# Order edges between VectorE and GpSimd, and ScalarE's copies in two halves, in an agent-attention and expert kernel

## The chip, the cores and the metric

The kernel runs on one core of a Trainium2 chip. The metric is device time in microseconds (us), the median of several executions. Five engines work side by side, each with its own instruction queue, which it works off in order: TensorE (PE in the profile), VectorE (DVE), ScalarE (ACT), GpSimd (POOL) and SyncE (SP, which issues most of the transfers). An instruction waits for others by semaphores, and what stands behind it on its engine waits with it.

## The reference

Agent attention over four batches of 10,048 tokens (128 channels, 49 agents), then one expert out of 16 for every token, which is picked in two steps (a group of four, then one of its four experts):

```python
a2k = softmax(scale * agents @ k^T)          # 4 x 49 x 10048
agent_v = a2k @ v                            # 4 x 49 x 128
x = softmax(scale * q @ agents^T) @ agent_v  # 4 x 10048 x 128
g = argmax(x @ w_group);  e = argmax(x @ w_expert[g])      # for each token
out = weight(g) * weight(e) * relu(x @ w1[g, e]) @ w2[g, e]   # 128 -> 1024 -> 128
```

The weights are the softmax values of the choices. q, k and agents are drawn eight times wider than v.

## The kernel before

Products run in f16 on TensorE, and precision is kept by splitting an f32 value into an upper f16 part and a lower one, the f16 of what the upper part leaves. For keys and queries (names `xf`, `xh`, `xl`) ScalarE copies the f32 chunk to `xh` and GpSimd takes `xl = xf - xh`, in pieces of 256 columns; a chunk has 10 tiles of 128 tokens, so 1,280 columns and five pieces. For values (`vf`, `vh`, `vl`) ScalarE writes `vh`, and **VectorE** takes `vl = 16 vf - vh` in two pieces of 640 columns; for the exponentials of the scores (`S`, `sh`, `sl`) GpSimd takes `sl = S - sh` in two pieces and adds `S` up in two more. For the exponentials of the queries (`ef`) GpSimd writes their lower part into `rows`. All of these read both operands from SBUF.

Batches come in the order 1, 2, 3, 0. The first 110 us or so do batch 1's attention. From then on to about 600 us TensorE works off *expert units*: for one of three batches at a time, and tiles of 512 tokens, eight units a tile. A unit is two products into PSUM (`ph`), an eviction by ScalarE (`hh`, relu) and by VectorE (`hl`, its lower part), and later three products `po`; up to eight units (`LAG`) lie between a unit's `ph` and its `po`. `ph` has three PSUM buffers, so TensorE waits when the evictions fall more than that behind. Between units `advance` puts steps of *lanes*, Python generators that do the attention of the following batches: `k1`, `k2`, `k3` (keys, then values), `q0` to `q3` (queries), `a0` to `a3` (weights, and in `pick` the choice of a batch's main expert), `p3` (scatter of rows). A lane that yields a number rests for so many units; how much of VectorE's and ScalarE's work goes between two units is held down by counts of it (`RATE`). The library's scheduler then orders each engine's queue by the data and order edges and a model of times of its own. So one more instruction, or one more yield, moves the order all over this stretch.

`pick` chooses a batch's main expert with a row of tiny VectorE instructions on 128 x 16 elements: `coe` is written, then multiplied in place by `cog` (both operands in SBUF), and so on to `cei`, the expert's number, by which SyncE loads its weights (`w1f`, `w2f`). This happens twice, for batches 2 and 3. From about 600 us the fourth batch, sorted by expert, is worked off.

`wide[0]` is True until the expert units begin. In the trace nearly all instructions of VectorE, ScalarE and TensorE carry line L140 (a helper that counts work), so they are told apart by the names of what they write and read.

Of the kernel before, what the change touches and what calls it, by code (L numbers as in the profile page):

```python
# [13 lines left out]
AF = mybir.ActivationFunctionType  # L14
ALU = mybir.AluOpType
# [5 lines left out]
P = 128  # L21
B = 4
N = 10048
C = 128
NA = 49
NG = 4
# [29 lines left out]
HT = CT // 2  # L56
VS = 16.0
# [21 lines left out]
HOP = 2  # L79
# [68 lines left out]
def build(ctx, tc, qT, kT, v, agT, wr, w1, w2, cpk, out, cols):  # L148
    nc = tc.nc
    pool, sync = nc.gpsimd, nc.sync  # L150
    work = np.zeros(3)
    pe = Counted(nc.tensor, work, 0, 4.0, 0.42)
    vec = Counted(nc.vector, work, 1, 65.0, 1.04)
    act = Counted(nc.scalar, work, 2, 190.0, 0.83)
# [19 lines left out]
    wide = [True]  # L174
# [101 lines left out]
    def split_load(kind, b, ci, early=None):  # L276
        t0, t1 = chunks[ci]
        n = (t1 - t0) * P if kind == "q" else min(N, t1 * P) - t0 * P
        if (kind, b, ci) in halves:
            lane("q0")["done"] += halves.pop("work") if "work" in halves else 0.0  # L280
            yield HOP
            return halves.pop((kind, b, ci))
        xf = loaded.pop((kind, b, ci), None) if early is None else first_loads[kind, ci]
        if early is not None and kind == "k" and ci < NB:
            xh = wbuf[ci].bitcast(F16)[:, 2 * CT * P:3 * CT * P]
            xl = early.tile([P, CT * P], F16, name="xs", bufs=4)
        elif early is not None and kind == "k" and ci > len(chunks) - 3:
            xh, xl = [early.tile([P, CT * P], F16, name="xs", bufs=4) for _ in range(2)]
        else:
            if xf is None:  # L290
                xf = load(kind, b, ci)
            xh = wk.tile([P, CT * P], F16, name="xh", tag="xh")
            xl = wk.tile([P, CT * P], F16, name="xl", tag="xl")
        act.activation(xh[:, 0:n], xf[:, 0:n], AF.Copy)
        if early is None:
            yield HOP
        a = 0
        if early is not None and kind == "k":
            a = min(n, SHARED)
            vec.tensor_sub(out=xl[:, 0:a], in0=xf[:, 0:a], in1=xh[:, 0:a])  # L300
        if a < n:
            for a in range(a, n, GP):
                z = min(n, a + GP)
                pool.tensor_sub(out=xl[:, a:z], in0=xf[:, a:z], in1=xh[:, a:z])  # L304
        return xh, xl

    chosen = []
# [9 lines left out]
    def paced(ins):  # L317

        tc.add_manual_dep(ins.ins, latest[0].ins.name, mybir.DependencyInfo(mybir.DependencyClass.Sync, mybir.DependencyReason.DATA),
                          reason="transfers are spread over the expert units")  # L320

    def skewed(n, *stages):

# [164 lines left out]
    def value_split(b, ci):  # L488

        st = state[b]  # L490
        vf = st.pop(("v", ci))
        sh, sl = [mo.tile([P, CT, NA], F16, name=name) for name in ("sh", "sl")]
        vh, vl = [wk.tile([P, CT * P], F16, name=name, tag="x" + name[1]).rearrange("p (t c) -> p t c", c=C) for name in ("vh", "vl")]
        parts = value_parts(b, ci)
        for x, y, m in parts:
            tc.keep_in_program_order(act.activation(vh[0:m, y], vf[0:m, y, 0:C], AF.Copy, scale=VS))
        yield 1
        for x, y, m in parts:
            act.activation(sh[0:m, y], x, AF.Copy)
        yield  # L500
        for x, y, m in parts:
            for a in range(0, x.shape[1], HT):
                z = slice(a, min(x.shape[1], a + HT))
                vec.scalar_tensor_tensor(out=vl[0:m, y][:, z], in0=vf[0:m, y, 0:C][:, z], scalar=VS, in1=vh[0:m, y][:, z], op0=ALU.mult, op1=ALU.subtract)
                yield
        yield 1
        for x, y, m in parts:
            for a in range(0, x.shape[1], HT):
                z = slice(a, min(x.shape[1], a + HT))
                pool.tensor_sub(out=sl[0:m, y][:, z], in0=x[:, z], in1=sh[0:m, y][:, z])  # L510
        for x, y, m in parts:
            for a in range(0, x.shape[1] if ci else 0, HT):
                z = slice(a, min(x.shape[1], a + HT))
                o = st["S"][0:m, y][:, z]
                pool.tensor_add(out=o, in0=o, in1=x[:, z])
        yield
        st["v", ci] = sh, sl, vh, vl

# [301 lines left out]
    def query_split(b, ci, x, early):  # L820
# [14 lines left out]
        x0 = st["rows", r][:, t0 - r * ST:t1 - r * ST]  # L835
        ef = x["ef"][:, 0:t1 - t0]
# [5 lines left out]
        if early:  # L842
            vec.tensor_sub(out=x0[:, :, NA:2 * NA], in0=ef, in1=x0[:, :, 0:NA])
        else:
            for a in range(0, t1 - t0, HT):
                z = min(t1 - t0, a + HT)
                pool.tensor_sub(out=x0[:, a:z, NA:2 * NA], in0=ef[:, a:z], in1=x0[:, a:z, 0:NA])  # L847
        st["split", ci] = True
        yield
        if b != SORTED and (t1 % ST == 0 or t1 == NT):  # L850
# [53 lines left out]
    def pick(b):  # L904
# [19 lines left out]
        og = sm.tile([P, NG], F32, name="cog")  # L924
# [3 lines left out]
        oe = sm.tile([P, NG, 4], F32, name="coe")  # L928
        vec.tensor_tensor(out=oe, in0=le, in1=em.unsqueeze(2).broadcast_to([P, NG, 4]), op=ALU.is_ge)
        yield  # L930
        vec.tensor_mul(out=oe, in0=oe, in1=og.unsqueeze(2).broadcast_to([P, NG, 4]))
        sc = sm.tile([P, NE], F32, name="csc")
        vec.tensor_sub(out=sc, in0=oe.rearrange("p g e -> p (g e)"), in1=eid)
        top = sm.tile([P, 1], F32, name="ctop")
# [917 lines left out]
```

## Time and profile before

| | |
|---|---|
| median of 3 runs | 914.24 us (911.54 to 914.42) |
| the profiled execution | 907.38 us, of which the profile's span is 905.1 us |
| TensorE busy, granted clock | 844.7 us (93%), 0.982 of full speed |
| VectorE, ScalarE, GpSimd busy | 710.8, 613.8 and 462.9 us (79%, 68%, 51%) |
| instructions | 22,546 |

Busy time is the union of an engine's instructions. An engine's idle time is put down to what ended it ("releaser"). TensorE's granted clock has two levels here, full speed (2.4 GHz, shown as 1.00) and half (1.2 GHz, 0.50); a stretch that has some of both shows a value between.

### The profile page before, as it was taken

The numbers are of one execution on the slowest core, as the hardware profiler recorded it, in microseconds if no ns is written. First come the engines' busy times: TensorE is split into PE (matmuls) and PEld (weight loads), VectorE is DVE, ScalarE is ACT, GpSimd is POOL, SyncE is SP. The second block draws the span as 40 slices with busy tenths as digits, with TensorE's granted clock in tenths as the row PEclk, the third lists the DMA queues.
The fourth block names the chain that finished last, engine by engine and source line by source line (L and its number), as shares of the span: only waits on it lengthen the run. The fifth ranks groups of instructions, "written<-read, shape, count | busy, mean of one in ns | idle before, by whom it ended". The sixth has DMA issues, their size and how long they took to land.

```text
span 905.1 us, 22546 instructions
## 1 busy us (share of the span) xinstructions
PE 844.7 (93%) x8668; PEld 502.2 (55%) x8669; DVE 710.8 (79%) x1442; ACT 613.8 (68%) x1078; POOL 462.9 (51%) x616
## 2 busy tenths in 40 slices
PE   4889999999797999898999999999999999999995
PEld 3745455555354555454455555554444477777775
DVE  7767898886799886688989689799977666766663
ACT  6568897867486777677678787766565555555552
POOL 4387495446426451838474343646555214444454
PEclk9989999999899999999999999999999999999998
DMA  9677436453554564434536222334756445555542
GB/s 360 245 244 272 139 108 225 157 163 128 173 170 130 169 196 147 156 115 152 169 112 242 83 75 104 112 102 151 230 176 212 138 140 165 174 190 187 176 141 98
DMA packets 58578, 149.95 MB, mean 166 GB/s; under 512 B 8702, under 2 KB 19830, under 8 KB 58460
## 3 DMA queue, kind: packets, MB, share of 16 engines
q1 hardware_dynamic: 53307, 138.11, 45.4%
q0 software_dynamic: 5152, 10.30, 3.2%
q8 instruction: 70, 1.15, 0.5%
q14 instruction: 49, 0.39, 0.1%
HBM read 108.33 MB, written 38.71 MB: 162 GB/s over the span
## 4 chain that ended last, share of the span: by engine, by line
PE 41%; DVE 8%; ACT 3%; DMA 2%; issue 2%; POOL 2%; POOLq 0%; ACTq 0%; DVEq 0%
PE po L140 24%; PE ph L140 12%; PE at L140 6%; DVE hl L140 3%; POOL xl L304 1%; ACT hh L140 1%; DMA out<-oo,er 1%; DVE vl L140 1%; DMA vf<-v 1%; DVE mq L140 1%; DVE ef L140 1%; ACT vh L140 1%; DVE oo L140 0%; POOL out L1485 0%; ACT es L140 0%
## 5 line engine op out<-in xcount | busy, mean ns | idle before, releaser
L140 DVE SCALAR_TENSOR_TENSOR hl<-ph,hh 128x512 f16<-128x512 f32 (+1 forms) x562 | 374.6, 677 | 125.7 <-ACT hh L140 122.0
L140 ACT ACTIVATE hh<-ph 128x512 f16<-128x512 f32 (+1 forms) x562 | 330.0, 594 | 188.2 <-PE ph L140 110.5
L140 PEld LDWEIGHTS <-wbuf 128*128 128x128 f16 (+2 forms) x2812 | 241.2, 97 | 282.6 <-issue 50.3
L140 PE MATMUL ph<-et,wbuf 98*128 98x512 f16 (+2 forms) x1048 | 317.4, 378 | 17.7 <-DVE hl L140 17.1
L140 PE MATMUL po<-hh,wbuf 128*128 128x512 f16 (+1 forms) x960 | 287.2, 379 | 0.0
L304 POOL TENSOR_TENSOR xl<-xf,xh 128x256 f16<-128x256 f32 x278 | 183.2, 696 | 137.1 <-ACT xh L140 124.4
L140 PE MATMUL po<-hl,wbuf 128*128 128x512 f16 (+1 forms) x480 | 181.3, 378 | 0.0
L1485 POOL DMA_INDIRECT out<-oo,er x82 | 80.7, 984 | 110.7 <-ACT hh L140 53.0
L140 PE MATMUL po<-wbuf,hh 128*128 128x128 f16 x1312 | 116.6, 219 | 0.0
L1199 POOL DMA_INDIRECT sorted_rows<-rows,slot x79 | 79.0, 1000 | 67.7 <-ACT hh L140 47.1
L140 PE MATMUL po<-wbuf,hl 128*128 128x128 f16 x656 | 112.9, 219 | 0.0
L140 PEld LDWEIGHTS <-hh 128*128 128x128 f16 x1312 | 99.2, 98 | 9.0 <-issue 9.0
L140 ACT ACTIVATE xh<-xf 128x1280 f16<-128x1280 f32 (+2 forms) x58 | 72.5, 1255 | 17.2 <-PE at L140 12.2
L510 POOL TENSOR_TENSOR sl<-S,sh 128x245 f16<-128x245 f32 (+2 forms) x51 | 37.8, 764 | 53.5 <-ACT sh L140 53.5
L140 PEld LDWEIGHTS <-hl 128*128 128x128 f16 x656 | 64.2, 98 | 0.0
L847 POOL TENSOR_TENSOR rows<-ef,rows 128x245 f16<-128x245 f32 (+1 forms) x62 | 39.9, 666 | 42.8 <-ACT rows L140 42.8
L140 PEld LDWEIGHTS <-xh 128*128 128x128 f16 x1166 | 46.3, 98 | 21.6 <-issue 2.2
L140 DVE SCALAR_TENSOR_TENSOR hl<-at,hh 128x512 f16<-128x512 f32 x82 | 55.8, 680 | 0.0
L140 DVE SCALAR_TENSOR_TENSOR vl<-vf,vh 128x640 f16<-128x640 f32 (+2 forms) x51 | 48.4, 956 | 7.2 <-ACT vh L140 7.2
L140 ACT ACTIVATE et<-at 98x512 f16<-98x512 f16 (+3 forms) x81 | 47.4, 596 | 8.8 <-PE at L140 8.7
L140 ACT ACTIVATE hh<-at 128x512 f16<-128x512 f32 x82 | 49.5, 604 | 0.0
L140 DVE TENSOR_TENSOR oo<-po,oo 128x512 f32<-128x512 f32 (+1 forms) x60 | 40.3, 672 | 9.6 <-PE po L140 6.2
(330 smaller groups left out, 1042.8 us busy)
## 6 DMA issues: line engine op xcount, KB each, us to landing
wbuf<-wdr SPq DMA_DIRECT2D x22, 832.0 KB
vf<-v SPq DMA_DIRECT2D x28, 645.0 KB
xf<-qT SPq DMA_DIRECT2D x27, 640.0 KB
xf<-kT SPq DMA_DIRECT2D x25, 640.0 KB
cols<-oo SPq DMA_DIRECT2D x60, 256.0 KB
oo<-cwt SPq DMA_DIRECT2D x57, 256.0 KB
erow<-rows SPq DMA_DIRECT2D x12, 490.0 KB
er<-sorted_rows SPq DMA_DIRECT2D x19, 256.0 KB
```

The source lines that it names most:

```text
L140: ins = f(*a, **k)
L304: pool.tensor_sub(out=xl[:, a:z], in0=xf[:, a:z], in1=xh[:, a:z])
L510: pool.tensor_sub(out=sl[0:m, y][:, z], in0=x[:, z], in1=sh[0:m, y][:, z])
L847: pool.tensor_sub(out=x0[:, a:z, NA:2 * NA], in0=ef[:, a:z], in1=x0[:, a:z, 0:NA])
L1199: ins = pool.indirect_dma_start(out=sorted_rows[:, :], out_offset=bass.IndirectOffsetOnAxis(ap=at, axis=0), in_=x, in_offset=None, bounds_ ...
L1485: ins = pool.indirect_dma_start(out=out, out_offset=bass.IndirectOffsetOnAxis(ap=to, axis=0), in_=y, in_offset=None, bounds_check=N - 1, o ...
```

## The change

`shared` marks GpSimd's pieces that read two operands from SBUF, and `by_itself` marks the `vl` pieces and the in-place product `coe` on VectorE. A `by_itself` instruction waits, by a semaphore edge, for the last `shared` piece that was issued before it in the program's order, unless another one has taken that edge; the next `shared` piece that is issued waits for the last `by_itself` instruction. Each mark is used up by its first taker. And after the opening, ScalarE's copy of a key or query chunk to `xh` is made in two halves of 640 columns, with a yield of one unit behind each, where one copy and a yield of two (`HOP`) stood.

```diff
-        act.activation(xh[:, 0:n], xf[:, 0:n], AF.Copy)
-        if early is None:
-            yield HOP
+        if early is None and not wide[0]:
+            for a in range(0, n, HT * P):
+                z = min(n, a + HT * P)
+                act.activation(xh[:, a:z], xf[:, a:z], AF.Copy)
+                yield 1
+            yield HOP - 1
+        else:
+            act.activation(xh[:, 0:n], xf[:, 0:n], AF.Copy)
+            if early is None:
+                yield HOP
...
-                pool.tensor_sub(out=xl[:, a:z], in0=xf[:, a:z], in1=xh[:, a:z])
+                shared(pool.tensor_sub(out=xl[:, a:z], in0=xf[:, a:z], in1=xh[:, a:z]))
...
+    lower, alone = [None], [None]
...
+    def follows(ins, other, reason):
+        tc.add_manual_dep(ins.ins, other.ins.name, mybir.DependencyInfo(mybir.DependencyClass.Sync, mybir.DependencyReason.DATA), reason=reason)
...
+    def shared(ins):
+
+        if alone[0]:
+            follows(ins, alone[0], "GpSimd pauses while VectorE reads both operands from SBUF")
+            alone[0] = None
+        if not wide[0]:
+            lower[0] = ins
+
+    def by_itself(ins):
+
+        if lower[0]:
+            follows(ins, lower[0], "VectorE reads both operands from SBUF when GpSimd pauses")
+            lower[0] = None
+        if not wide[0]:
+            alone[0] = ins
...
-                vec.scalar_tensor_tensor(out=vl[0:m, y][:, z], in0=vf[0:m, y, 0:C][:, z], scalar=VS, in1=vh[0:m, y][:, z], op0=ALU.mult, op1=ALU.subtract)
+                by_itself(vec.scalar_tensor_tensor(out=vl[0:m, y][:, z], in0=vf[0:m, y, 0:C][:, z], scalar=VS, in1=vh[0:m, y][:, z], op0=ALU.mult, op1=ALU.subtract))
...
-                pool.tensor_sub(out=sl[0:m, y][:, z], in0=x[:, z], in1=sh[0:m, y][:, z])
+                shared(pool.tensor_sub(out=sl[0:m, y][:, z], in0=x[:, z], in1=sh[0:m, y][:, z]))
...
-                pool.tensor_add(out=o, in0=o, in1=x[:, z])
+                shared(pool.tensor_add(out=o, in0=o, in1=x[:, z]))
...
-                pool.tensor_sub(out=x0[:, a:z, NA:2 * NA], in0=ef[:, a:z], in1=x0[:, a:z, 0:NA])
+                shared(pool.tensor_sub(out=x0[:, a:z, NA:2 * NA], in0=ef[:, a:z], in1=x0[:, a:z, 0:NA]))
...
-        vec.tensor_mul(out=oe, in0=oe, in1=og.unsqueeze(2).broadcast_to([P, NG, 4]))
+        by_itself(vec.tensor_mul(out=oe, in0=oe, in1=og.unsqueeze(2).broadcast_to([P, NG, 4])))
```

**The first choice of an expert.** GpSimd's queue before, where batch 2's `coe` is made on VectorE (numbers are buffers; "waits" names the engines and transfers whose semaphores an instruction waits for; x4 stands for four equal instructions):

```order
L847 TENSOR_TENSOR rows_3995<-ef_3824,rows_3995 128x5x49
L304 TENSOR_TENSOR xl_3795<-xf_3739,xh_3794 128x256 [waits DMAHW6_49,PE_49,Activation_49]
L304 TENSOR_TENSOR xl_3795<-xf_3739,xh_3794 128x256 x4
L304 TENSOR_TENSOR xl_3862<-xf_3807,xh_3861 128x256 [waits DMAHW6_49,PE_49,Activation_49]
L304 TENSOR_TENSOR xl_3862<-xf_3807,xh_3861 128x256 x4
L304 TENSOR_TENSOR xl_3957<-xf_3876,xh_3956 128x256 [waits DMAHW7_49,PE_49,Activation_49]
L304 TENSOR_TENSOR xl_3957<-xf_3876,xh_3956 128x256 x4
L304 TENSOR_TENSOR xl_4056<-xf_3977,xh_4055 128x256 [waits DMAHW0_49,PE_49,Activation_49]
L304 TENSOR_TENSOR xl_4056<-xf_3977,xh_4055 128x256 x4
```

And the same place of GpSimd's queue in the changed kernel:

```order
L311 TENSOR_TENSOR xl_3696<-xf_3597,xh_3695 128x256 x2
L875 TENSOR_TENSOR rows_4037<-ef_3851,rows_4037 128x5x49 [waits DMAHW3_49,Activation_49]
L875 TENSOR_TENSOR rows_4037<-ef_3851,rows_4037 128x5x49
L311 TENSOR_TENSOR xl_3776<-xf_3698,xh_3775 128x256 [waits DMAHW4_49,Activation_49]
L311 TENSOR_TENSOR xl_3776<-xf_3698,xh_3775 128x256 [waits Activation_49]
L311 TENSOR_TENSOR xl_3776<-xf_3698,xh_3775 128x256 x2
L311 TENSOR_TENSOR xl_3776<-xf_3698,xh_3775 128x256 [waits DVE_49]
L311 TENSOR_TENSOR xl_3566<-xf_3290,xh_3565 128x256 [waits DMAHW6_49,PE_49,Pool_49]
```

The first piece of the chunk `xl_3776` now stands behind the other four and waits for VectorE (for `coe`). VectorE's queue there, before and changed:

```order
L140 TENSOR_TENSOR oo_3591<-po_3593,oo_3591 128x512 [waits DMAHW7_49,DMAHW5_49,PE_49]
L140 TENSOR_REDUCE cem_3910<-at_3836 128x4
L140 TENSOR_TENSOR coe_3912<-at_3836,cem_3910 128x16 [waits DVE_49]
L140 TENSOR_TENSOR coe_3912<-coe_3912,cog_3908 128x16 [waits DVE_49]
L140 SCALAR_TENSOR_TENSOR hl_3897<-ph_3893,hh_3896 128x512 [waits Activation_49]
```

The same product in the changed kernel, which waits for GpSimd as well:

```order
L140 TENSOR_REDUCE cem_3823<-at_3752 128x4
L140 TENSOR_TENSOR coe_3825<-at_3752,cem_3823 128x16 [waits DVE_49]
L140 TENSOR_TENSOR coe_3825<-coe_3825,cog_3821 128x16 [waits DVE_49,Pool_49]
L140 TENSOR_TENSOR csc_3828<-coe_3825,cp_97 128x16 [waits DVE_49]
L140 TENSOR_REDUCE ctop_3830<-csc_3828 128x1 [waits DVE_49]
```

GpSimd's piece for which it waits is the last of `xl_3696`, two chunks ahead of it in program order.

**A value chunk's lower parts.** GpSimd's queue before at the first value chunks of batch 3; `sl` waits for ScalarE (`sh`) alone:

```order
L847 TENSOR_TENSOR rows_3995<-ef_4338,rows_3995 128x5x49
L510 TENSOR_TENSOR sl_4465<-S_3565,sh_4464 128x245 [waits Activation_49]
L510 TENSOR_TENSOR sl_4465<-S_3565,sh_4464 128x245
L515 TENSOR_TENSOR S_3565<-S_3565 128x245 [waits Pool_49] x2
L515 TENSOR_TENSOR S_3565<-S_3565 128x245 [waits Activation_49,Pool_49]
```

The same chunks of the changed kernel:

```order
L538 TENSOR_TENSOR sl_4793<-S_3592,sh_4792 128x245 [waits Activation_49]
L543 TENSOR_TENSOR S_3592<-S_3592 128x245 [waits Activation_49,Pool_49]
L543 TENSOR_TENSOR S_3592<-S_3592 128x245 [waits Pool_49]
...
L862 MEMSET rows_5878 128x98 [waits PE_49]
L875 TENSOR_TENSOR rows_4978<-ef_4874,rows_4978 128x5x49 [waits Activation_49]
L538 TENSOR_TENSOR sl_4793<-S_3592,sh_4792 128x245 [waits DVE_49]
L538 TENSOR_TENSOR sl_4906<-S_3592,sh_4905 128x245 [waits PE_49]
```

The first piece of `sl_4793` has moved behind the second, and waits for VectorE's `vl_4795`, the same chunk's.

**The load of batch 3's expert.** SyncE's queue before, and in the changed kernel:

```order
L1465 DMA oo_8119<-cwt1_141 128x512 [waits DMAHW7_49,DMAHW6_49,DMAHW1_49]
L1304 TENSOR_LOAD cei_7879 [waits DVE_49]
L1307 ISA
L1307 DMA w1f_8007<-w1 128x1024 [waits DMAHW0_49,Activation_49,Pool_49]
L1308 ISA
L1308 DMA w2f_8008<-w2 128x8x128 [waits DVE_49,Activation_49]
```

The changed kernel's, where the load takes the buffer that the chunk `xl_7406` gives back:

```order
L1493 DMA oo_8334<-cwt1_141 128x512 [waits DMAHW7_49,DMAHW0_49]
L1332 TENSOR_LOAD cei_7638 [waits DVE_49]
L1335 ISA
L1335 DMA w1f_7747<-w1 128x1024 [waits Pool_49]
L1336 ISA
L1336 DMA w2f_7748<-w2 128x8x128 [waits DMAHW3_49,DMAHW2_49,Activation_49]
```

And GpSimd's queue there in the changed kernel:

```order
L538 TENSOR_TENSOR sl_7863<-S_5984,sh_7862 128x147
L538 TENSOR_TENSOR sl_7863<-S_5984,sh_7862 64x49 [waits Activation_49]
L311 TENSOR_TENSOR xl_7406<-xf_7136,xh_7405 128x256 [waits DMAHW0_49,PE_49]
L311 TENSOR_TENSOR xl_7406<-xf_7136,xh_7405 128x256 x3
L311 TENSOR_TENSOR xl_7406<-xf_7136,xh_7405 128x256 [waits DVE_49]
```

The piece that gives the buffer free waits for VectorE's `vl_7865`; before, the load waited for pieces that stood far ahead of it.

## Rows read from the trace of the kernel before

**Rows 1.** Busy time by stage: us, each engine's busy us (instructions), clock, DMA.

```profile
110.00:600.00 490.00, 459.94 (x4541) 252.09 (x4541) 409.34 (x796) 368.49 (x641) 261.75 (x383) 0.98 0.44 147
600.00:880.00 280.00, 280.00 (x2820) 178.96 (x2819) 208.84 (x430) 162.48 (x303) 128.85 (x130) 1.00 0.51 170
```

**Rows 2.** TensorE's waits from 110 to 600 us: total us, times, longest.

```profile
PE ph L140 <- DVE hl L140: 16.7, 12, 5.6
PE at L140 <- POOL xl L304: 6.3, 7, 2.8
PE at L140 <- DVE vl L140: 1.5, 3, 0.6
```

**Rows 3.** TensorE's timeline: start, us, what; in brackets idle time before, releaser.

```profile
226.18 0.28 PE L140 MATMUL at<-agh,xl 128*128 128x49 f16 x5
232.03 1.01 PE L140 MATMUL ph<-et,wbuf 98*128 98x512 f16 x2 [5.56 <-DVE hl L140]
...
289.00 0.80 PE L140 MATMUL ph<-et,wbuf 98*128 98x384 f16 x2 [2.44 <-DVE hl L140]
...
383.97 0.30 PE L140 MATMUL at<-agh,xl 128*128 128x49 f16 x5 [2.81 <-POOL xl L304]
...
430.48 0.59 PE L140 MATMUL ph<-et,wbuf 98*128 98x512 f16 x2 [3.24 <-DVE hl L140]
```

**Rows 4.** VectorE's timeline at four places.

```profile
172.47 0.82 DVE L140 SCALAR_TENSOR_TENSOR vl<-vf,vh 128x640 f16<-128x640 f32 x1 [0.47 <-ACT vh L140]
...
224.15 7.22 DVE L140 TENSOR_TENSOR coe<-coe,cog 128x16 f32<-128x16 f32 x1
...
284.91 3.57 DVE L140 SCALAR_TENSOR_TENSOR vl<-vf,vh 128x640 f16<-128x640 f32 x1
...
447.86 2.46 DVE L140 SCALAR_TENSOR_TENSOR vl<-vf,vh 128x640 f16<-128x640 f32 x2
```

**Rows 5.** GpSimd's timeline around the same places, and at 375 us.

```profile
218.73 12.61 POOL L304 TENSOR_TENSOR xl<-xf,xh 128x256 f16<-128x256 f32 x20
...
283.47 3.18 POOL L304 TENSOR_TENSOR xl<-xf,xh 128x256 f16<-128x256 f32 x5
286.61 1.19 POOL L510 TENSOR_TENSOR sl<-S,sh 128x245 f16<-128x245 f32 x2
...
375.70 9.47 POOL L304 TENSOR_TENSOR xl<-xf,xh 128x256 f16<-128x256 f32 x15 [4.08 <-ACT xh L140]
...
447.80 1.84 POOL L510 TENSOR_TENSOR sl<-S,sh 128x245 f16<-128x245 f32 x2 [4.89 <-ACT sh L140]
```

**Rows 6.** Busy time behind the long waits, columns as in rows 1.

```profile
231.00:237.50 6.50, 5.47 (x27) 2.35 (x27) 6.21 (x22) 1.76 (x4) 0.34 (x1) 0.50 0.32 85
...
289.00:292.00 3.00, 3.00 (x25) 1.88 (x25) 3.00 (x6) 0.95 (x2) 0.00 (x0) 0.50 0.56 157
...
384.50:387.90 3.40, 3.40 (x23) 1.67 (x22) 2.02 (x4) 2.42 (x5) 3.40 (x7) 0.50 0.69 216
```

**Rows 7.** Groups by form from 110 to 600 us: busy us, mean ns, idle before.

```profile
L140 DVE SCALAR_TENSOR_TENSOR vl<-vf,vh 128x640 f16<-128x640 f32 x45 | 45.6, 1019 | 7.2 <-ACT vh L140 7.2
L140 DVE TENSOR_TENSOR coe<-coe,cog 128x16 f32<-128x16 f32 x2 | 7.5, 3775 | 0.1
...
L140 ACT ACTIVATE hh<-ph 128x512 f16<-128x512 f32 x316 | 186.3, 598 | 60.1 <-PE ph L140 57.5 <-DVE hl L140 0.9
L140 ACT ACTIVATE xh<-xf 128x1280 f16<-128x1280 f32 x36 | 45.7, 1272 | 15.5 <-PE at L140 11.1 <-POOL xl L304 2.4 <-DVE vl L140 1.0
...
L304 POOL TENSOR_TENSOR xl<-xf,xh 128x256 f16<-128x256 f32 x204 | 136.2, 704 | 120.5 <-ACT xh L140 108.2 <-PE at L140 9.8 <-DMA vf<-v 2.5
```

**Rows 8.** First load of an expert's weights, and TensorE's wait for it.

```profile
45.82 0.36 SPq L1307 DMA_DIRECT2D w1f<-w  x1
...
49.52 2.05 PE L140 MATMUL at<-w1f,at 128*128 128x512 f32 x2 [0.66 <-DMA w1f<-w]
```

**Rows 9.** `sl` over the whole span: duration ns min/median/max, first and last start.

```profile
L510 POOL TENSOR_TENSOR sl<-S,sh x51: 271/647/1286, 111.2 to 456.9; 128x245 f16<-128x245 f32 x45, 128x147 f16<-128x147 f32 x3, 64x49 f16<-64x49 f32 x3
```

## The prediction

> **What bounds the kernel now.** I read the busy time by stage first. From 600 to 880 us TensorE is busy all of the time, and from 110 to 600 us, where the change is at work, for 459.94 of 490 us [rows 1]: what can be won is the 30 us that TensorE idles there, and what half clock adds to them. VectorE is busy for 409 us of that stretch and ScalarE for 368, so neither is a bound over the whole, but each works its queue off in order, and one late instruction holds all that stand behind it. TensorE's own waits there come next: 16.7 us for `hl`, VectorE's eviction, in only twelve waits, and 6.3 us for GpSimd's `xl` [rows 2]. TensorE's timeline shows that four waits make up most of it, of 5.56, 2.44, 2.81 and 3.24 us [rows 3].
>
> I then looked at what VectorE did in the first two. From 224.15 us it spent 7.22 us on `coe`, a product of 16 columns whose other instance in the stretch took 0.3 us (two of mean 3,775 ns), and from 284.91 us 3.57 us on a `vl` piece that takes 0.82 where GpSimd is idle [rows 4, 7]. GpSimd was running pieces without a break: twenty `xl` from 218.73 to 231.34 us, and five `xl` and two `sl` from 283.47 to 287.80 [rows 5]. `coe` ended when the last of the twenty had ended, `vl` 0.68 us after the last `sl`. VectorE's instruction with two operands in SBUF was held for as long as GpSimd's back-to-back pieces lasted. In most other places it lost only the piece that was running: at 447.86 us two `vl` took 2.46 us where 1.64 are due, and GpSimd's two `sl` took 1.84 us in sum [rows 4, 5]. The third long wait is GpSimd's backlog itself, 15 pieces in a row from 375.70 us [rows 5], and the fourth I put down to neither part of the change.
>
> A long wait costs a second time. Behind the first, TensorE's granted clock was 0.50 for 6.5 us, behind the second for 3.0, behind the third for 3.4 [rows 6], and TensorE was busy there, so half of that is lost: 3.2, 1.5 and 1.7 us.
>
> **The change part by part.** The sum is made against the profiled execution's 907.4 us (span 905.1). The median of the runs is 914.24, 6.8 us above it, and I carry the difference over.
>
> *`coe` (gain).* Wait and clock are 5.56 + 3.2 = 8.8 us. In the changed queue `coe` waits for the last piece of a chunk that stands ahead of two `rows` pieces and four `xl` pieces, and the next piece after these waits for `coe`. So GpSimd can no longer run past it: at worst those six pieces lie in the way, at 12.61 / 20 = 0.63 us each, 3.8 us; at best nothing. The `ph` buffers cover a little over a unit, and most of the six are issued well ahead, so I take 1.3 us as left: -7.5. Bounds -8.8 and -4.
>
> *The long `vl` (gain).* 2.44 + 1.5 = 3.9 us. Only the first piece issued behind a `vl` is tied to it; the other four of an `xl` chunk are not, and in the changed queue they now stand ahead of the tied one. So a burst beside `vl` can come again, only shorter: -2.5, bounds -3.9 and 0.
>
> *The other `vl` (gain).* 45 pieces at 1,019 ns against 0.82 us are 9.0 us too much [rows 7, 4], of which the long one is 2.75. The other 6.2 us lie on VectorE and mostly under the three `ph` buffers; what reaches TensorE is near the 1.5 us that it waits for `vl` by name [rows 2]: -1.5, bounds 0 and -4.
>
> *Copies in halves.* A copy of 512 columns takes 598 ns and one of 1,280 takes 1,272 [rows 7], so 0.88 ns a column, and a half of 640 about 0.71 us by that line (an estimate). GpSimd may start 0.56 us sooner, and of TensorE's seven waits for `xl` I count four that begin with a fresh copy: 4 x 0.56, -2.0, bounds 0 and -6.3 - 1.7 = -8. ScalarE pays 2 x 0.71 - 1.27 = 0.15 us for each of 52 copies, 7.8 us. That lies in its idle quarter (368.49 of 490 us busy) and costs nothing as long as the halves go between evictions; without that cover it is up to +7.8. In the other direction, an eviction is held by a copy for 0.71 us at most where it was 1.27, which I put at nothing since no long wait of TensorE goes back to it.
>
> *GpSimd's `sl` behind `vl` (loss).* Before, `sl` ran beside `vl` and nobody waited for it: TensorE's waits for GpSimd name `xl` alone [rows 2]. Now the first piece of `sl` starts when the chunk's last `vl` has ended, and TensorE's first product with it reads just that piece. So `sl` comes up to 0.82 us later plus its own 0.65 [rows 4, 9]. There are 24 value chunks, and in the changed queue TensorE's first product with `sl` stands within a unit of the delayed piece in eight. I take 0.4 us each, +3; bounds 0 and 8 x 1.47 = 12. What is queued behind the piece on GpSimd, further `sl`, `S` sums and `xl`, is late by the same.
>
> *VectorE behind GpSimd (loss).* 12 of the `vl` and one `coe` wait for a piece of GpSimd's. Ten of the pieces are issued many units ahead; in two cases the piece stands directly ahead of the `vl`, behind a chunk of five pieces, 5 x 0.63 = 3.2 us. Behind the `vl` stand `hl` evictions, for which TensorE waits. +1.5, bounds 0 and 6.4.
>
> *The load of batch 3's expert (loss).* It now waits for the buffer of `xl_7406`, whose last piece waits for the last `vl` of batch 3. The first such load was issued at 45.82 us, and TensorE waited for it until 49.52, 3.7 us later [rows 8]. In the changed queue TensorE has other work between the issue and the product that needs the load, which I put at half of that: +2, bounds 0 and 3.7 + 1.7 for a half clock behind it = 5.4.
>
> *The new order elsewhere.* The extra instructions and yields move side work between units over the whole stretch, so waits such as those at 383.97 and 430.48 us [rows 3] may go or come again elsewhere. I take nothing for it, and up to 6 us either way in the range.
>
> The sum: -7.5 - 2.5 - 1.5 - 2.0 + 3 + 1.5 + 2 = -7.0 us. The profiled execution would come to about 900, the median to **907**.
>
> **A rule against a row.** At `coe` the row shows a wait through eleven or more pieces of GpSimd's [rows 4, 5]. The Trainium skill (SBUF — State Buffer, Who interferes with whom) says that a VectorE instruction with two SBUF inputs contends with a GpSimd instruction that reads SBUF, and that whichever comes second is blocked until the first has finished. That two such instructions exclude each other agrees with the rows; that the loser waits for one instruction does not: by that rule `coe` would have lost at most one piece, 0.66 us.
>
> **The rivals.**
> *GpSimd's pauses become the bound (slower).* The place is the value chunks: `sl` behind `vl`, and the `xl` of the other lane behind both, in a queue that had bursts of 9.47 and 12.61 us without a break [rows 5], in which every pause is handed on. If all 24 chunks lose the 0.65 us of a piece, that is 15.6 where I took 3, and the sum is +5.6; 920, and with one half clock more 921 to 922. It decides from about 0.42 us a chunk: 24 x 0.42 = 10 is what the gains of 13.5 leave after the other losses of 3.5. For it speaks that nothing on TensorE's side was moved back to make room; against it, that TensorE waited for `vl` only three times in 24 chunks [rows 2], so its products with values mostly come later than their operands.
> *The exclusion leaks (no change).* Four of five `xl` pieces stay untied. If `coe` and `vl` meet bursts as before, the gains of 11.5 us shrink to 4 or so, the copies' 2 and the losses of 6.5 stay, and it ends at 912 to 917. Against it: at `coe` the queue is fenced by a tied piece.
> *One piece only.* If VectorE loses but the piece that runs, then the 7 us of `coe` have a cause that the edges don't touch; the edges give 4.0 at most, and with the copies and the losses, -4.0 - 2.0 + 6.5, it ends near 915. The rows of GpSimd's burst, whose end is `coe`'s end within 0.03 us, speak against it. This is what the rule of the Trainium skill above would make of the change.
> *More is gained.* `xl` is late no more either, and the long waits at 383.97 and 430.48 us go too, the first with the half clock behind it [rows 6]: 2.8 + 1.7 + 3.2 = 7.7 us more, 894 to 902, or a little below.
>
> **How the numbers follow.** 907 has a chance of 0.46 with a range of its own of 902 to 911.5; more gained 0.18; the leak 0.14 and one piece only 0.04, both ending within 0.3% (911.5 to 917), which is about what a measurement of this kernel can tell from no change; GpSimd's pauses 0.18. So faster 0.64, same 0.18, slower 0.18. The range of 897 to 919 leaves out the better half of the fourth case and the worse half of the slower one.
>
> **What would show it.** Right: `coe` under 2 us in both places, no `vl` over 1.5 us, GpSimd's pieces beside them at 0.65 us and not 1.2, no half clock between 215 and 245 us, `xl` pieces starting within 0.75 us of their copy's start, and TensorE idle for 20 to 25 us from 110 to 600 us. Wrong: TensorE's waits name `sl`, or `w1f`'s load, for more than 6 us together; a `hl` that waits behind a `vl` which waits for GpSimd; or a new wait of over 2 us with half clock behind it at a place where before had none.

## The result and the profile after

The changed kernel took 918.8 us (median of 20 runs, 913.16 to 925.81), the kernel before, timed beside it, 912.97 us (20 runs, 908.84 to 915.33). The ratio is 1.0072 with a 95% interval of 1.0052 to 1.0091: slower by 0.7%, where I had forecast 0.8% faster. Its profiled execution has a span of 915.0 us against 905.1.

Busy time by stage, with the columns of [rows 1]:

```profile
110.00:600.00 490.00, 457.10 (x4466) 249.27 (x4464) 398.27 (x786) 367.19 (x675) 258.08 (x383) 0.98 0.45 145
600.00:880.00 280.00, 279.37 (x2796) 176.77 (x2794) 208.80 (x433) 162.48 (x303) 129.91 (x132) 1.00 0.51 170
215.00:245.00 30.00, 29.29 (x322) 16.06 (x320) 23.35 (x50) 23.73 (x45) 22.94 (x38) 1.00 0.65 208
281.60:285.00 3.40, 3.24 (x24) 1.92 (x25) 0.56 (x1) 2.14 (x3) 1.83 (x4) 0.50 0.62 195
428.40:435.10 6.70, 5.74 (x40) 2.82 (x40) 2.89 (x7) 1.26 (x3) 2.06 (x5) 0.50 0.59 222
476.20:479.50 3.30, 3.30 (x6) 1.20 (x6) 0.96 (x3) 1.59 (x3) 3.30 (x6) 0.50 0.73 234
```

TensorE idles 33 us from 110 to 600 us, where it idled 30. The place of the first choice, 215 to 245 us, now has under 1 us of idle time and no half clock. But half clock stands in the last three stretches, each behind one of the new waits below, and over the whole stretch the granted clock is 0.98 in both kernels: as much half clock came as went. TensorE's waits from 110 to 600 us say who is waited for:

```profile
PE ph L140 <- DVE hl L140: 6.3, 8, 2.2
PE at L140 <- POOL sl L538: 5.5, 5, 2.4
PE at L140 <- DVE ef L140: 4.3, 2, 2.6
PE at L140 <- POOL rows L875: 3.4, 1, 3.4
PE at L140 <- POOL xl L311: 2.7, 4, 1.4
PE at L140 <- DVE cwo L140: 2.0, 2, 1.0
PE at L140 <- DMA w1f<-w: 1.7, 1, 1.7
```

Against [rows 2] the waits for `hl` fell by 10 us and those for `xl` by more than half. New are 8.9 us for GpSimd's `sl` and `rows` and 1.7 us for the expert's weights, and the waits for `ef` are 4.3 us where they were 1.4. VectorE's timeline shows the product of the choice at both places, and the instruction behind which `ef` came late:

```profile
222.06 0.17 DVE L140 TENSOR_TENSOR coe<-coe,cog 128x16 f32<-128x16 f32 x1
...
453.22 0.61 DVE L140 TENSOR_TENSOR coe<-coe,cog 128x16 f32<-128x16 f32 x1
...
513.02 0.11 DVE L140 MEMSET xf<- 128x64 f32 x1 [4.51 <-POOL xl L311]
```

TensorE's timeline has the four new long waits:

```profile
281.76 0.45 PE L140 MATMUL at<-ident,rows 128*98 128x128 f16 x2 [3.43 <-POOL rows L875]
...
429.36 0.20 PE L140 MATMUL at<-sl,vh 128*128 128x49 f16 x1 [2.44 <-POOL sl L538]
...
475.93 1.91 PE L140 MATMUL at<-w1f,at 128*128 128x512 f32 x2 [1.68 <-DMA w1f<-w]
...
515.00 0.42 PE L140 MATMUL at<-ident,rows 128*98 128x128 f16 x4 [2.55 <-DVE ef L140]
```

Now GpSimd's timeline ahead of the second of them (`sl` at 429.36 us):

```profile
419.26 3.15 POOL L311 TENSOR_TENSOR xl<-xf,xh 128x256 f16<-128x256 f32 x4
422.38 0.65 POOL L538 TENSOR_TENSOR sl<-S,sh 128x245 f16<-128x245 f32 x1
422.99 1.85 POOL L543 TENSOR_TENSOR S<-S 128x245 f32<-128x245 f32 x2
424.80 0.66 POOL L311 TENSOR_TENSOR xl<-xf,xh 128x256 f16<-128x256 f32 x1
425.42 3.28 POOL L543 TENSOR_TENSOR S<-S 128x245 f32<-128x245 f32 x5
428.67 1.79 POOL L538 TENSOR_TENSOR sl<-S,sh 128x245 f16<-128x245 f32 x3
```

GpSimd worked without a pause. The `sl` at 422.38 is the chunk's second piece; the first, tied to `vl` and the one that TensorE's product reads, is the first of the three at 428.67. The edge had long let it go: VectorE's last `vl` ahead of it began at 425.48 us and took 0.80, so it ended 2.4 us before the piece began. The piece was late because of **where it stood**, behind seven sums and an `xl` piece. In the changed queue 14 of the 24 value chunks have their first piece tied, and in all 14 it comes last of its chunk.

Groups by form, as [rows 7]: a `vl` piece takes 0.1 us less than before on average, and a half copy takes what was estimated and a little more:

```profile
L140 ACT ACTIVATE xh<-xf 128x640 f16<-128x640 f32 x78 | 56.9, 736 | 22.9 <-PE at L140 13.8 <-DMA xf<-kT 3.7 <-PE ph L140 2.3
L140 DVE SCALAR_TENSOR_TENSOR vl<-vf,vh 128x640 f16<-128x640 f32 x45 | 41.3, 920 | 6.6 <-ACT vh L140 5.7 <-POOL xl L311 0.7
```

To see where time went although the order differs, I added up the product work that TensorE had done (columns at full clock, 55 ns a product at least) from the matmul records, and compared when two kernels reach the same amount. Time lost against before in each stretch, in us (minus is time won; stretches in before's time; good to about 1 us):

| kernel | to 95 | 95-210 | 210-240 | 240-440 | 440-486 | 486-602 | later |
|---|---|---|---|---|---|---|---|
| changed | 0.6 | 4.8 | -8.5 | -6.6 | 10.4 | 4.6 | 3.2 |
| edges alone, e1 | 0.1 | 5.9 | -7.9 | 2.8 | 3.8 | 0 | 0 |
| coe's edges, e3 | 0.7 | 0.6 | -7.9 | 1.2 | 0 | 0 | 0.1 |
| xl edges, e7 | 1.8 | 1.6 | -7.8 | -5.3 | 2.5 | 0 | 0 |
| coe's edges and halves, e8 | 3.6 | 8.0 | -8.1 | -10.7 | 12.1 | 1.8 | 0.9 |
| all edges, pieces in order, e17 | -0.8 | 3.4 | -8.0 | -6.5 | 6.0 | 0.3 | 5.7 |
| the same, `rows` too, e18 | 0.5 | 3.1 | -7.8 | -6.8 | 6.8 | -0.1 | 1.4 |

Every kernel of the table, all with `coe`'s edges, wins 8 us at the first choice. What differs is what it loses elsewhere.

### The profile page after: what moved, and what is told of

Read it like the earlier page. It is cut to its first block, busy times and chain, and to the rows that moved or that the text cites. A ratio compares the mean times of both kernels' runs of the same rounds, so it can differ in the third digit from the quotient of the medians.

```text
span 915.0 us, 22589 instructions
## 1 busy us (share of the span) xinstructions
PE 845.7 (92%) x8668; PEld 501.5 (55%) x8669; DVE 702.9 (77%) x1442; ACT 616.2 (67%) x1130; POOL 461.2 (50%) x616
## 4 chain that ended last, share of the span: by engine, by line
PE 59%; DVE 11%; issue 9%; POOL 9%; ACT 8%; DMA 3%; SPq 0%; POOLq 0%; DVEq 0%; ACTq 0%
PE po L140 31%; PE ph L140 17%; PE at L140 11%; POOL xl L311 4%; DVE hl L140 4%; ACT hh L140 3%; POOL S L543 2%; ACT xh L140 1%; POOL sl L538 1%; POOL out L1513 1%; DVE S L140 1%; DVE vl L140 1%; ACT S L140 1%; POOL rows L875 1%; DVE oo L140 1%
## 5 line engine op out<-in xcount | busy, mean ns | idle before, releaser
L311 POOL TENSOR_TENSOR xl<-xf,xh 128x256 f16<-128x256 f32 (+1 forms) x278 | 183.3, 693 | 113.1 <-ACT xh L140 107.2
L140 ACT ACTIVATE xh<-xf 128x640 f16<-128x640 f32 (+1 forms) x110 | 82.1, 757 | 23.4 <-PE at L140 14.2
L538 POOL TENSOR_TENSOR sl<-S,sh 128x245 f16<-128x245 f32 (+2 forms) x51 | 33.8, 682 | 72.7 <-ACT sh L140 51.3
L140 DVE SCALAR_TENSOR_TENSOR vl<-vf,vh 128x640 f16<-128x640 f32 (+2 forms) x51 | 44.5, 879 | 6.6 <-ACT vh L140 5.7
```

The lines of the kernel that those rows point to most:

```text
L140: ins = f(*a, **k)
L311: shared(pool.tensor_sub(out=xl[:, a:z], in0=xf[:, a:z], in1=xh[:, a:z]))
L538: shared(pool.tensor_sub(out=sl[0:m, y][:, z], in0=x[:, z], in1=sh[0:m, y][:, z]))
```

## The experiments

Two theories stood at the start. A: the edges win, and the order that the halves bring loses. B: the edges themselves lose, because GpSimd pauses. Ratios below are to the kernel before, timed beside each group of runs on the same chip, with their 95% intervals. It took 907.9 to 909.1 us beside e1 to e16, but 917.89 us beside e17 and e18.

**e1: the edges without the halves.**

```diff
-        if early is None and not wide[0]:
-            for a in range(0, n, HT * P):
...
+        act.activation(xh[:, 0:n], xf[:, 0:n], AF.Copy)
+        if early is None:
+            yield HOP
```

> The order edges alone, the copies whole as before, so nearly before's order. Theory A (the edges do what they are for, and the loss comes with the new order that the halves bring): coe takes under 1 us in both places, the wait of 5.56 us at 232 us and the half clock behind it go, and with the long vl's part the time is 901 to 906 us, 0.7 to 1.3% faster than before. Theory B (the edges pause GpSimd, and its late sl and rows pieces cost more than the edges win): TensorE's waits name sl and rows for 8 us or more together, and the time is 912 to 920 us, equal or slower.

Measured: 1.0028 (1.0009 to 1.0046), 911.04 us. The first half of theory A held (`coe`, 8 us won) and its sum didn't. TensorE's waits name `sl` and `rows` for 9.0 us, as B said:

```profile
PE at L140 <- POOL xl L304: 9.9, 10, 2.8
PE ph L140 <- DVE hl L140: 8.6, 7, 3.4
PE at L140 <- POOL sl L531: 6.6, 4, 3.9
PE at L140 <- POOL rows L868: 2.4, 2, 1.5
```

The `hl` of 3.4 us goes back to GpSimd as well: VectorE stood idle ahead of `mx` for 3.53 us until GpSimd's last `S` sum came, with `hl` queued behind it:

```profile
132.53 0.98 DVE L140 TENSOR_REDUCE mx<-S 128x49 f32<-128x490 f32 x1 [3.53 <-POOL S L536]
```

**e2: the halves without the edges** (before, with the copy's loop of the change).

> The copies in halves with their yields alone, no order edges. Theory A: slower than before, 916 to 925 us, with no edge in the program, and new waits of TensorE at places where before had none. Theory B: 905 to 912 us, since xl starts sooner and nothing pauses GpSimd. How long coe takes here says whether its long wait of before hangs on where GpSimd's bursts happen to fall: over 4 us if it is met by one again, under 1 us if the new order alone moved it away.

Measured: 1.0105 (1.0082 to 1.0127), 915.93 us; `coe` took 5.6 us at one place. The halves lose with no edge in the program, so B alone doesn't hold either. TensorE waits 4.3 us for `ef` here too, so in the changed kernel that wait comes with the halves and not with the edges.

**e3: only `coe` is tied.**

```diff
-                by_itself(vec.scalar_tensor_tensor(out=vl[0:m, y][:, z], ...))
+                vec.scalar_tensor_tensor(out=vl[0:m, y][:, z], ...)
```

> Only the product of the choice excludes GpSimd's pieces; the vl pieces run beside GpSimd as before, the copies are whole. By both theories the first long wait and the half clock behind it go (8.8 us by the sum on record), 903 to 907 us. Theory A: within 2 us of the kernel with all edges, since the other edges cost and win little. Theory B: faster than that kernel by 5 us or more, since only here GpSimd isn't paused at the value chunks.

Measured: 0.9936 (0.9918 to 0.9953), 902.18 us. So 0.92 points lie between it and all edges: theory B's line, 5 us or more.

**e4: all edges, whole copies, a rest of three units.**

```diff
-            yield HOP
+            yield HOP if wide[0] else HOP + 1
```

> All edges and whole copies, but the lane rests three units behind a copy instead of two, as many steps as the changed kernel's two halves and their rests take. If the cost lies in the longer lanes (each of 52 chunks one unit later, so that the values of the last batch, the load of its expert and the scatter come later and are crowded): 913 to 920 us, near the changed kernel. If it lies in what the halves themselves do on ScalarE: 901 to 908 us, near the kernel with edges alone. A time between the two leaves it to the order as such.

Measured: 1.0082 (1.0058 to 1.0105), 915.97 us. That looked like the longer lane as the halves' cost; e9 took it back.

**e5 and e6: one direction of the `vl` edges each**, on top of `coe`'s. In e5 `vl` waits for GpSimd and is not waited for; e6 is the reverse (`both` is False for `vl`; in e6 it guards the other edge).

```diff
-        if not wide[0]:
+        if not wide[0] and both:
             alone[0] = ins
```

> The kernel with coe's edges, and of the vl edges only those by which VectorE waits for GpSimd (no piece of GpSimd's waits for a vl). Every engine's order is that of the kernel with coe's edges alone. Theory A now (the vl edges lose where GpSimd's tied piece of sl or rows goes behind its sums, late for TensorE's product): within 2 us of the kernel with coe's edges, 0.992 to 0.996 of before. Rival (VectorE's own waits for GpSimd hold the hl evictions behind them): 3 us or more above it, 0.997 or more.

> The other direction alone: coe's edges, and GpSimd's first piece behind a vl waits for it, but no vl waits for GpSimd. Theory A: the loss is here, 1.000 to 1.005 of before, with TensorE waiting for sl and rows for 6 us or more, as with all edges. Rival: 0.992 to 0.996, as with coe's edges alone.

Measured: e5 0.9935 (0.9923 to 0.9947), the same as e3; VectorE's own waits cost nothing. e6 1.0024 (1.0009 to 1.0038), the same as all edges. The loss hangs on the edges by which GpSimd's pieces wait for `vl`.

**e7 and e12: which pieces.** In e7 only the `xl` pieces are `shared`; in e12 `xl` and `rows`.

```diff
-                shared(pool.tensor_sub(out=sl[0:m, y][:, z], ...))
+                pool.tensor_sub(out=sl[0:m, y][:, z], ...)
```

> All edges in both directions, but only the xl pieces of keys and queries take part; sl, the S sums and rows are free as before. Theory A: the waits for sl and rows are gone, and the time is within 3 us of the kernel with coe's edges alone, 0.992 to 0.998. Rival (any pause of GpSimd's costs, whichever piece it falls on): 1.000 to 1.005, with TensorE's waits for xl longer in place of those for sl.

> All edges, but of the value chunks' pieces neither sl nor the S sums take part; the xl pieces and the rows pieces do. If the loss of the full set lies in sl and the sums behind it: 0.989 to 0.993, as with xl alone (0.9903). If the rows pieces of the queries are late by the edges just so: 0.997 or more, with TensorE's waits for rows of 3 us or more.

Measured: e7 0.9903 (0.9887 to 0.9919), 899.73 us, with no wait of TensorE for `sl` or `rows` left. e12 0.999 (0.9973 to 1.0007), with 2.4 us of waits for `rows` and the same `mx` behind late sums (2.87 us) as in e1. So the set with `rows` is 0.87 points slower than `xl` alone, and leaving `sl` and the sums untied wins only 0.38 of the 1.25 points between e1 and e7. That it is the late `rows` pieces that cost the rest isn't shown: the sums ahead of `mx` are late here although they aren't tied, and e17 wins with `rows` tied as before. Ties on `xl` win 0.33 points here over `coe`'s edges alone. With the halves they win too (e14 under e8, e16 under e11), and with a rest of three units they lose 0.54 (e13 over e9).

**e17 and e18: every edge kept, the pieces' order restored.** In e17 each piece of a value chunk follows the one before it in program order (`sl`, `sl`, sums); e18 does so for the two `rows` pieces as well. Otherwise they are e1.

```diff
-                shared(pool.tensor_sub(out=sl[0:m, y][:, z], ...))
+                ins = pool.tensor_sub(out=sl[0:m, y][:, z], ...)
+                if behind:
+                    follows(ins, behind, "in order")
+                shared(ins)
+                behind = ins
```

> All edges on both engines and whole copies, as in the kernel of edges alone (1.0028), and besides GpSimd's pieces of a value chunk follow each other in program order, so that the tied sl piece stays first instead of going behind the second one, sums and other chunks' pieces (in 15 of 16 tied chunks it stood last before). If the edges lose by that place in the queue: 0.990 to 0.997, and TensorE's waits for sl under 2 us. If they lose because GpSimd really stands and waits for vl: 1.001 to 1.006, with idle time of GpSimd behind vl growing.

> The same, and the two rows pieces of a query chunk follow each other as well. If the place in the queue is the cause for rows too: 1 to 4 us below the kernel with the value chunks alone in order, with TensorE's waits for rows under 1 us. By real pauses as the cause: no better than it.

Measured: e17 0.9916 (0.9885 to 0.9946), e18 0.9883 (0.9845 to 0.9921). With all edges in place the loss turned into a gain of 0.8 to 1.2% over the kernel before as it ran beside them. The size is less sure than the sign. In their own time, 909.59 and 907.17 us, they are no faster than the kernel before was beside the other runs. The traces don't depend on that. Up to 602 us e17 is 5.6 us and e18 4.3 us ahead of the trace of before, where e1 is 4.7 us behind it. From there on e17 loses 5.7 us in the table, and TensorE has waits that neither before nor e1 has behind 600 us:

```profile
PE ph L140 <- SPq L1529: 2.3, 1, 2.3
PE po L140 <- issue: 1.2, 4, 0.4
```

So the traces put the gain nearer to 0.5%. GpSimd's idle time behind VectorE, in e1:

```profile
POOL sl L531 <- DVE vl L140: 36.8, 9, 8.2
POOL rows L868 <- DVE vl L140: 3.2, 2, 2.4
```

and in e17:

```profile
POOL sl L532 <- DVE vl L140: 39.4, 10, 8.3
POOL rows L877 <- DVE vl L140: 1.5, 2, 0.8
```

GpSimd pauses just as long, so pausing by itself is not what lost. TensorE's waits in e17:

```profile
PE at L140 <- POOL xl L304: 9.8, 10, 2.8
PE ph L140 <- DVE hl L140: 4.3, 8, 1.1
PE at L140 <- POOL rows L877: 2.7, 3, 1.0
PE at L140 <- POOL sl L532: 2.5, 3, 1.5
```

`sl` fell from 6.6 to 2.5 us (under 2 was expected) and `hl` halved. Against e1 three places win most, in e1's time: 5.3 us at 128 to 140 us, where VectorE stood ahead of `mx`; 4.3 us at 424 to 430 us, where TensorE waited 3.9 us for `sl`; and 4.8 us at 285 to 295 us, where a `vl` took 3.0 us in e1 and none is over 1.33 here. The second is the tied `sl`, late by its place. The first is the place of the sums, which e12 has late too with the sums untied, and the third a burst beside `vl` that e17's order misses. About 5 us are lost again at other places. So the chain mends more than the tied `sl` alone. GpSimd's timeline in e17 at the place of the changed kernel's long wait has the pairs together and ahead of the sums:

```profile
420.54 1.32 POOL L532 TENSOR_TENSOR sl<-S,sh 128x245 f16<-128x245 f32 x2
421.94 1.31 POOL L541 TENSOR_TENSOR S<-S 128x245 f32<-128x245 f32 x2
423.21 1.41 POOL L532 TENSOR_TENSOR sl<-S,sh 128x245 f16<-128x245 f32 x2
```

e18 against e17 is within the intervals. That order is restored for `rows` too may give 2 or 3 us; it isn't shown. TensorE still waits 2.2 us for `rows` there, where under 1 was expected, and in e17 the tied `rows` pieces stand as far back as in e1.

**e8 to e11: the halves, on top of `coe`'s edges alone.** e8 has them as in the change; e10 leaves out the yield behind the second half, so that the rest is two units in all; e11 has both halves back to back, then `yield HOP`; e9 is e4's rest of three units with whole copies.

```diff
                 act.activation(xh[:, a:z], xf[:, a:z], AF.Copy)
-                yield 1
+                if z < n:
+                    yield 1
             yield HOP - 1
```

> Copies in halves as in the changed kernel, and of the edges only coe's. If the halves' cost is their own (1.05% in the run of halves alone, which still had a coe of 5 us or so in it): 0.998 to 1.004, that is 4 to 10 us above the kernel with coe's edges and whole copies. If halves alone lost only by the burst that coe met there: 0.990 to 0.995.

> Coe's edges, whole copies, and the lane rests three units behind a copy instead of two. If what the halves cost (0.9 points, from 0.9936 to 1.0025) is the one unit by which they lengthen a lane's chunk: 1.000 to 1.004. If it lies in the halves themselves, their number on ScalarE or their places: 0.992 to 0.996.

> Coe's edges and copies in halves with one unit between the halves and one behind the second, two in all as before. By the longer lane as the cause: 0.992 to 0.996, as with whole copies, or lower where xl starts sooner. By the halves themselves: 1.000 to 1.004.

> Coe's edges, and the two halves right behind each other with the rest of two units behind the second, so that only the count of ScalarE's instructions and the earlier start of xl differ from whole copies. If an instruction more for each chunk on ScalarE costs by itself: 0.998 or more. If the loss lies in the units and places: 0.990 to 0.996.

Measured: e8 1.0025 (1.0006 to 1.0044), e9 0.9898 (0.9876 to 0.992), e10 0.9982 (0.9967 to 0.9996), e11 0.9967 (0.9953 to 0.9982). All three forms of halves are above e3's 0.9936, and the longer rest with whole copies is below it, so a longer lane isn't the cost. e8 shows one way in which the halves' order lost, on VectorE and on GpSimd:

```profile
469.48 5.85 DVE L140 SCALAR_TENSOR_TENSOR vl<-vf,vh 128x640 f16<-128x640 f32 x2 [0.30 <-ACT vh L140]
```

```profile
467.87 6.31 POOL L311 TENSOR_TENSOR xl<-xf,xh 128x256 f16<-128x256 f32 x10
```

Two chunks' pieces ran back to back, and a `vl` (5.38 us of the 5.85) was held until they ended. In e10 and e11 a `vl` of 4.4 and 5.4 us stands at other places.

**e13 to e16: more orders.** e13: e7's edges, a rest of three; e14: e7's edges and the change's halves; e15: `coe`'s edges, a rest of one; e16: e7's edges, halves back to back.

```diff
-            yield HOP
+            yield HOP if wide[0] else HOP - 1
```

> Edges between the xl pieces and VectorE only (the set that gave 0.9903), whole copies, a rest of three units. If the two gains add up (0.4 points each over coe's edges alone): 0.984 to 0.989, the fastest so far. If each is a draw of the order: anywhere from 0.988 to 0.998.

> The changed kernel without the edges on sl, the S sums and rows: copies in halves with its yields, edges of the xl pieces only. If the halves cost something of their own in whatever order: 0.3 to 1.0 points above whole copies with the same edges, 0.993 to 1.001. If the five losses with halves so far were draws of the order: as likely below 0.9903 as above.

> Coe's edges, whole copies, a rest of one unit: one more order of the same instructions. It says how far an order alone moves the time with whole copies: if little, 0.989 to 0.995, and then 0.997 to 1.0025 with halves is outside of it; if as much as the halves, a time of 0.997 or more here.

> Edges of the xl pieces only, the two halves right behind each other and a rest of two units. By a cost of the halves' own: 0.993 to 0.998, above the 0.9903 of whole copies. By the order as a draw: below 0.9903 with a chance of one half.

Measured: e13 0.9952 (0.9938 to 0.9966), e14 0.9977 (0.9959 to 0.9995), e15 0.9993 (0.9981 to 1.0005), e16 0.9941 (0.9925 to 0.9957). The gains of e7 and e9 don't add up. Halves lose against whole copies with the same edges in seven pairs of seven (changed to e1, e2 to before, e8, e10 and e11 to e3, e14 and e16 to e7), by 0.31 to 1.05 points, 0.61 on average. Another rest with whole copies loses in three of four (e4 against e1, e13 against e7, e15 against e3; e9 wins against e3), 0.31 on average, and the two sets overlap (e16 is below e13 and e15). So about half of what the halves lose is what a new order of this stretch loses in these runs; that they cost something of their own is neither shown nor excluded.

What a good and a bad order differ in can be read from all twenty traces: TensorE's idle time from 95 to 600 us plus half of its time at half clock. The four fastest kernels (e18, e9, e7, e17) have 28 to 33 us of it, with one idle stretch of over 2 us each; the five slowest (e8, e1, the changed one, e4, e2) have 43 to 48 us, with three to five. So an order wins or loses by a few long waits and the half clock behind them.

## Why the prediction was wrong

The step that failed first is **GpSimd's `sl` behind `vl`**, and with it the tied `rows` pieces, for which I had no term. I priced `sl` as a wait (up to 0.82 us and the piece's own 0.65, in eight chunks, +3). e5 to e7 put the loss on the edges by which `sl`, the `S` sums and `rows` wait for `vl`, at 1.25 points of 909 us between e7 and e1, some 11 us, near the term's upper bound. With halves it is 0.95 points (the changed kernel less e14). And the mechanism was another one: e17 and e18 keep all these edges and are 9 to 10 us ahead of e1 at 602 us. The library's scheduler sets a tied piece behind whatever it can issue first, so the first `sl` went behind its pair, sums and other chunks. I had shown such a row ahead of the prediction, with the first piece moved behind the second, and still priced the wait and not the place. A lucky order of e17 and e18 is a rival that no run excludes; but another order of the same work won 0.38 points at most in the eleven pairs below. How the 11 us divide between `sl`, the sums and `rows` stays open: by e12 `sl` and the sums are 0.38 points and `rows` 0.87, and e17 wins with `rows` tied. TensorE's waits in e1 name `sl` for 6.6 us and `rows` for 2.4.

The second is **the new order elsewhere**, set at 0 with 6 us either way. Eleven kernels with another order of the same work lost in ten cases, 0.5 points on average (4.5 us). I read it as an order that fits having more to lose than to win, so that the middle of this term was not 0. Eight of the eleven are held against e3 or e7, which came out fast themselves, so part of the 0.5 may be the choice of these two.

From the runs, the change adds up so (points of 909 us): `coe`'s edges -0.64, the `xl` and `vl` edges -0.33 (e7 less e3), `sl`, `S` and `rows` +1.25 (e1 less e7), halves +0.44 (changed less e1), in sum +0.72, each known to some 0.2 or 0.3. It is one chain of kernels, so it must add up, and another chain splits it otherwise: by e14 the halves are +0.74 and `sl`, `S` and `rows` +0.95.

The other steps:
- **`coe`**: right. The 7.22 us of the first choice became 0.17 (the second took 0.61 where it was 0.33), the wait and the half clock went, and 7.8 to 8.5 us were won at the place in the table, against -7.5.
- **The long `vl`**: the leak that I feared. In e1, e6 and e7 it is still there with 2.9 to 3.0 us, behind untied `xl` pieces; it left little gain in these. In the changed kernel no `vl` is over 1.66 us, and in e17 and e18 none over 1.33.
- **The other `vl`**: their sum fell by 45.6 - 41.3 = 4.3 us; what of it reaches TensorE can't be told apart from the order.
- **Copies in halves**: the gain itself was right, TensorE's waits for `xl` fell from 6.3 to 2.7 us (2.5 in e2, without edges). Where an `xl` waited for its copy, it starts 0.81 us after the copy's start instead of 1.35 (medians from the records); 0.56 sooner was forecast, 0.53 came. ScalarE's 736 ns a half are 0.2 us a pair more than a whole copy, near the 0.15. What took it back, the new order or a cost of the halves' own, stays open, as said above.
- **VectorE behind GpSimd**: +1.5 was too much; e5 equals e3.
- **The load of batch 3's expert**: +2 forecast; the wait was 1.68 us, with 3.3 us of half clock behind it, of which half is lost, so 3.3 in sum.

Of the rivals, *GpSimd's pauses become the bound* had the place, the direction and nearly the time (920 against 918.8), but not the cause: GpSimd pauses as much in e17, which doesn't lose. Of the signs named for a wrong forecast, two came: waits for `sl` and `w1f` of 7.2 us together, and waits of over 2 us with half clock behind them at new places. A `hl` behind a waiting `vl` did not.

A better version than both kernels comes out of it: `xl` edges alone (e7, 0.9903), `coe`'s edges with a rest of three (e9, 0.9898), or all edges with the pieces kept in order (e18, 0.9883, against the kernel before at 917.89 us). Their intervals touch; which is best isn't settled. In their own time e7 and e9 took 899.73 and 900.92 us, e18 907.17.

## What to carry to other kernels

An order edge given to a scheduler does two things: the tied instruction waits, and here it was also set behind everything that could go first; look up its new place in the queue, ask who reads its result next, and chain it to its neighbours if it must stay ahead of them. Tie only the instructions that are known to hurt each other. And when a change reorders a stretch that already fits, expect the order itself to move the time, more often up than down in these runs, and time each part alone before the sum.

## What the hardware showed that I had not expected

A VectorE instruction with two operands in SBUF was held through a whole burst of GpSimd's at more than one odd place: a `vl` took 5.38 us beside ten `xl` pieces in e8, 5.37 in e2, 5.43 in e11, 3.0 in e1. The Trainium skill (SBUF — State Buffer, Who interferes with whom) has the second comer of two such instructions blocked until the first has finished; by that each would have lost one piece of 0.65 us or so. These rows disagree, and so do the runs: taking the burst away from `coe` won 8 us. But most rows agree with it. Over all twenty traces 141 `vl` pieces of 640 columns began when three or more `xl` pieces in a row, the running one counted, were still to end on GpSimd; 12 of them took 3.0 us or more, and none of the other 129 over 1.37. The kernel before has this one:

```profile
309.87 1.34 DVE L140 SCALAR_TENSOR_TENSOR vl<-vf,vh 128x640 f16<-128x640 f32 x1 [1.44 <-ACT vh L140]
```

```profile
308.60 3.78 POOL L304 TENSOR_TENSOR xl<-xf,xh 128x256 f16<-128x256 f32 x5 [4.40 <-PE at L140]
```

It lost one piece although the burst went on until 312.38 us. What decides between the two isn't shown by these traces.

The same wait had two outcomes for the clock. In e1 and e3 TensorE waits 1.58 us for the same `xl` pieces, at 244.46 and 239.72 us. In e1 (245 to 251.6 us):

```profile
245.00:251.60 6.60, 6.36 (x34) 2.84 (x33) 4.42 (x8) 1.78 (x4) 3.42 (x7) 0.50 0.70 225
```

and in e3 (239.5 to 246 us):

```profile
239.50:246.00 6.50, 6.01 (x53) 3.30 (x54) 5.80 (x11) 3.50 (x8) 4.20 (x8) 1.00 0.62 191
```

That is some 3 us of difference behind an equal wait, which I can't explain from these traces; it is part of why orders that look alike differ.
